# Output of tiles 0 to 11 made transposed, with x transposed as its residual

## The chip, the core and the metric

The kernel runs on one core of a Trainium2 chip. The time is that of the device in microseconds. Before the change it is 268.86 us, the median of 3 runs (268.37 to 268.89). Besides, one execution was recorded by the profiler; every duration below that is not a median comes from that one.

## What is computed

One layer with two branches over the same normalised input, summed with the input itself. S = 2048 tokens, D = 640 features, H = 32 heads of Dh = 20, F = 1536.

```python
xn = _layernorm(x)
# branch A: linear attention
q, k, v = split_heads(xn @ wqkv)
pq = einsum("bhsd,hdf->bhsf", q, w_phi)          # pk from k in the same way
phi_q = concat([softmax(pq), softmax(-pq)])      # phi_k from pk in the same way
kv  = einsum("bhsf,bhsd->bhfd", phi_k, v);  z = sum_s(phi_k)
o   = (phi_q @ kv) / (phi_q . z + 1e-6)
# branch B: gated MLP
h   = silu(xn @ w1) * (xn @ w3)
out = x + o @ wo + h @ w2
```

Inputs and output are bf16.

## The kernel before

The order of the instructions is written out by hand: each engine (TensorE, VectorE, ScalarE, GpSimd, SyncE) works through its own list in the order of the program, and waits where an operand or a buffer is not there yet. All transfers, transposing ones too, are issued by SyncE, one after the other; a transfer whose condition isn't met holds up those behind it.

Tokens are worked in 16 tiles of 128. The normalised input stands transposed in `xnT` (features by tokens). The units of work:

- `phi_unit` (L396) makes the features phi of one tile: 10 matmuls (L342, tile `pk` or `pq`) into two PSUM banks, six exponentials on ScalarE (L371), a sum (L405) and a reciprocal (L407) on VectorE, and a product on GpSimd (L408), which finishes phi.
- `kv_unit` (L481) adds one tile's phi and v into `acc`, 11 matmuls (L485).
- `glu_unit` (L439) makes one block of 128 rows of h for 512 tokens: five matmuls for the gate and five for up (L444, 512 columns each), into two PSUM banks; then a tanh on ScalarE (L455) and two products on VectorE, `gs` (L472, which reads the gate's bank) and the one into `hT` (L475, which reads the other). There are 48 such units; `fill(n)` issues the next n of them.
- `phi_transposed` (L510) transposes phi of a tile by DMA; `r_unit` (L515) multiplies it with kv (11 matmuls, L520) and `quotient` divides (L536 to L541) into `o_`; `o_transposed` (L564) transposes o of that tile by DMA into `oT`, which holds four tiles.
- `out_unit` (L575) makes the output of one tile: for each of 17 steps (12 of h with `w2`, 5 of o with `wo`), the tile's h or o is the stationary operand and 320 columns of the weight the moving one, twice, so 34 matmuls (L583) into two banks. VectorE adds the residual `xr` (L592), which `residual` has loaded, and the tile is stored.

PSUM has six banks that take turns (`bank`), and one pair beside them (`pair`).

The first loop (L822) goes over the 16 tiles for k; its passes are called i here. A pass is one `phi_unit`, one `kv_unit` (from i=2, for the tile of two passes before) and two GLU units (one in i=0). Passes 4 to 8 also fuse a block of weights and sum up one column block of the v weights on ScalarE (`column_sum`, L317). In pass 9 these sums are written to DRAM (`row`) and read back, broadcast to all partitions (`wide`, here called `less_sum`); the second transfer waits for the first. From pass 10 on, VectorE uses them in `raw_centred` (L325), one tile a pass for four passes, behind the products of that pass's GLU units.

The second loop (L846) goes over the tiles for q; its passes are called t. Pass t does `phi_unit(t)`, `r_unit(t-2)` and, from t=4, `out_unit(t-4)`; passes 0 to 3 do two GLU units each in place of the output. `w2` is loaded in pass 1. A flag (is the softmax safe without its maximum?) is made by VectorE in t=6 (L625, `flag_unit`) and read by the engines in t=8 (L878); if it is 0, a second, safer program is run, which does not happen with these inputs. The last tile's output is made in two parts, 384 and 256 columns, each stored at once.

Of the kernel before, what the change touches and what calls it, by code (L numbers as in the profile page):

```python
# [8 lines left out]
P = 128  # L9
# [3 lines left out]
def kernel(  # L13
# [17 lines left out]
    nc = tc.nc  # L31
    bf = mybir.dt.bfloat16
    f32 = mybir.dt.float32
    AF = mybir.ActivationFunctionType
    ALU = mybir.AluOpType
    AX = mybir.AxisListType

    _, S, D = A_x.shape
    H, Dh = 32, 20
    F = B_w1.shape[1]  # L40
    NST, NSC, KD, KF = S // P, S // 512, D // P, F // P
# [17 lines left out]
    x2 = A_x[0]  # L59
    out2 = out[0]  # L60
# [6 lines left out]
    def bank(name, dt=f32):  # L67
        n = 512 if dt == f32 else 1024
        return psum.tile([P, n], dt, name=name, tag="bank")
# [5 lines left out]
    xnT = one.tile([P, KD, S], bf, name="xnT")  # L75
    wkphi = one.tile([P, KD, D], bf, name="wkphi")
    wqphi = one.tile([P, KD, D], bf, name="wqphi")
    w1 = one.tile([P, KD, F], bf, name="w1")
    w3 = one.tile([P, KD, F], bf, name="w3")
# [26 lines left out]
    oT = reg_v[:, KF * D : KF * D + KD * 512].rearrange("p (c s) -> p c s", c=KD)  # L106

    def slot(i):  # L110
        return phi[:, i].rearrange("p c g f -> p (c g f)")
# [6 lines left out]
    v_raw = one.tile([P, RAW, D], f32, name="v_raw")  # L118
    less_sum = wide[:, 0:D]
    flat = v_raw[:].rearrange("p t d -> p (t d)")[0:1, 0 : P * 8]  # L120
    sums = one.tile([P, KD], f32, name="sums")
    drift = one.tile([P, RAW], f32, name="drift")
    dram = ctx.enter_context(tc.tile_pool(name="dram", bufs=1, space=bass.MemoryType.DRAM))
# [4 lines left out]
    def ld(dst, src):  # L128
        nc.sync.dma_start(out=dst, in_=src)
# [9 lines left out]
    with tc.manual_schedule():  # L139
# [193 lines left out]
        def tile_of(t):  # L333
            return slice(t * P, (t + 1) * P)
# [104 lines left out]
        def glu_unit(sc, fi, banks=None):  # L439

            gp, up = banks or (bank("gp")[:], bank("up")[:])
            for ps, w in ((gp, w1), (up, w3)):
                for c in range(KD):
                    nc.tensor.matmul(  # L444
                        ps,
                        w[:, c, fi * P : (fi + 1) * P],
                        xnT[:, c, sc * 512 : (sc + 1) * 512],
                        start=(c == 0),
                        stop=(c == KD - 1),
                    )  # L450
            return glu_done(sc, fi, gp, up)

        def glu_done(sc, fi, gp, up):
            th = work.tile([P, 512], f32, name="th")
            nc.scalar.activation(out=th[:], in_=gp, func=AF.Tanh, scale=0.5)  # L455
            return lambda: glu_product(sc, fi, gp, up, th)
# [104 lines left out]
                in1=den[:, :, None].to_broadcast([P, H, Dh]),  # L561
            )

        def o_transposed(t):  # L564
            tau = t % 4
            nc.sync.dma_start_transpose(
                out=oT[:, :, tau * P : (tau + 1) * P], in_=o_[:, t % 2]
            )

        def residual(rows):  # L570
            xr = work.tile([P, D], bf, name="xr")
            ld(xr[:], x2[rows, :])
            return xr

        def out_unit(h, ocols, xr, last=None):  # L575

            acc = [bank("acc"), bank("acc")]
            rows = [(h[:, k], w2[:, k]) for k in range(KF)]
            rows += [(oT[:, k, ocols], wo[:, k]) for k in range(KD)]
            res = work.tile([P, D], bf, name="res")  # L580

            def product(j, ps, a, b):
                nc.tensor.matmul(  # L583
                    ps[:, 0 : b - a],
                    rows[j][0],
                    rows[j][1][:, a:b],
                    start=(j == 0),
                    stop=(j == len(rows) - 1),
                )

            def result(ps, a, b):
                nc.vector.tensor_tensor(  # L592
                    out=res[:, a:b], in0=ps[:, 0 : b - a], in1=xr[:, a:b], op=ALU.add
                )

            if last is None:
                parts = [(acc[i], i * HD, (i + 1) * HD) for i in range(2)]
                for j in range(len(rows)):
                    for part in parts:
                        product(j, *part)  # L600
                for part in parts:
                    result(*part)
                return res
            for part in ((acc[0], 0, 384), (acc[1], 384, D)):
                for j in range(len(rows)):
                    product(j, *part)
                result(*part)
                a, b = part[1:]
                ld(out2[last, a:b], res[:, a:b])

        norms = one.tile([P, 8], f32, name="norms")
        flag = one.tile([P, 1], mybir.dt.int32, name="flag")

# [24 lines left out]
        def fill(n):  # L640
            for _ in range(n):
                glu_unit(*glu.pop(0))()

        def stats(t0, n):
            ln_stats(*range(t0, t0 + n))
# [176 lines left out]
        for i, t in enumerate(turns):  # L822
            phi_unit(t, wkphi, "pk")
            if i > 1:
                kv_unit(turns[i - 2], vaug[:, turns[i - 2]], acc, i == 2, False)
            if i:
                fill(1)
            if 4 <= i < 9:
                fuse(wqphi, wqT, i - 4, [bank("pf"), bank("pf")])
            fill(1)  # L830
            if i == 0:
                nc.sync.dma_start_transpose(out=wvT, in_=A_wqkv[:, 2 * D : 3 * D])
            if 4 <= i < 9:
                column_sum(i - 4)
            if i == 9:
                ld(row[:].rearrange("c p -> p c"), sums[:])
                ld(less_sum, row[:].rearrange("c p -> (c p)").partition_broadcast(P))
            if 10 <= i < 10 + RAW:
                raw_centred(i - 10)
            if i >= 12:  # L840
                norm_unit(wkphi, 0, i - 12)
        ld(wo, A_wo.rearrange("(c p) d -> p c d", p=P))

        for t in range(NST + 4):  # L846
            if t < NST:
                phi_unit(t, wqphi, "pq")
            if t < 2:
                kv_unit(turns[t - 2], vaug[:, turns[t - 2]], acc, False, t == 1)  # L850
                if t == 1:
                    kv_done([acc[:, 0], acc[:, 1]])
                    ld(w2, B_w2.rearrange("(c p) d -> p c d", p=P))
            if t < 4:
                fill(2)
            else:
                last = tile_of(NST - 1) if t == NST + 3 else None
                res = out_unit(hT[:, t - 4], tile_of(t % 4), xr, last)
            if 2 <= t < NST + 2:
                r_unit(t - 2)  # L860

            if 3 <= t < NST + 3:
                xr = residual(tile_of(t - 3))
            if 4 <= t < NST + 3:
                ld(out2[(t - 4) * P : (t - 3) * P, :], res[:])
            if t < NST:
                phi_transposed(t)
            if 2 <= t < NST + 2:
                o_transposed(t - 2)
            if t < 4:  # L870
                norm_unit(wqphi, 1, t)
            if t == 4:
                ld(listed[:], norms[:])
                ld(flat, listed[:].rearrange("p g -> (p g)").partition_broadcast(1))
            if t == 6:
                flag_unit()
            if t == 8:
                ok = nc.values_load(flag[0:1, 0:1], min_val=0, max_val=1)  # L878


# [53 lines left out]
```

## Time and profile before

| | us |
|---|---|
| median of 3 runs | 268.86 |
| the profiled execution | 268.62 |
| its span, first to last instruction | 266.8 |
| TensorE busy (modelled) | 262.0, 98% |
| VectorE busy | 195.0, 73% |
| ScalarE busy | 114.8, 43% |
| GpSimd busy | 91.1, 34% |
| queue of all transfers, share of 16 DMA engines | 46.9% |
| granted TensorE clock | 0.998 |

A matmul's reported length holds its way through the array, so matmuls overlap in the table (379 ns for one of 512 columns); what one of them costs in a dense stream is read from the starts of the matmuls that follow each other.

The span in 40 slices of 6.67 us shows where the stages lie. Each digit is the busy share of a slice in tenths:

```profile
PE   8999999999999999999999999999999999999995
PEld 7766565655555555555555555677777777777773
DVE  4779984398766777779998699976877777776341
ACT  5784444744466666344556665422222222221000
POOL 5052520055333333333444333333344444333000
PEclk9999999999999999999999999999999999999999
DMA  6998856976000000060000098455655555556931
```

Slices 0 to 7 load and normalise; the first loop runs from about 50 us (slice 7) to 144.6 us (slice 21), with nearly no transfers; the second from there to the end, with transfers at about half of what the DMA engines can hold.

### The profile page before, as it was taken

What the parts mean: (1) busy time and instruction counts of PE and PEld (TensorE: products, weight loads), DVE (VectorE), ACT (ScalarE), POOL (GpSimd) and SP (SyncE); (2) the same over time, 40 slices, a digit from 0 to 9 for tenths busy, and PEclk for the clock granted to TensorE, in tenths of its full rate; (3) what the DMA queues carried; (4) which work ended last, traced back from release to release, by engine and by line L of the source; (5) the groups of instructions that cost most, each with busy time, mean ns of one, the idle gap of its engine ahead of it and who ended that gap; (6) DMA issues with size and microseconds to landing.
All of it is one profiled execution on the core that took longest, in us unless ns stands there. A gap on an engine that the chain in (4) does not pass through costs nothing.

```text
span 266.8 us, 5294 instructions
## 1 busy us (share of the span) xinstructions
PE 262.0 (98%) x1979; PEld 167.7 (63%) x1997; DVE 195.0 (73%) x363; ACT 114.8 (43%) x348; POOL 91.1 (34%) x88
## 2 busy tenths in 40 slices
PE   8999999999999999999999999999999999999995
PEld 7766565655555555555555555677777777777773
DVE  4779984398766777779998699976877777776341
ACT  5784444744466666344556665422222222221000
POOL 5052520055333333333444333333344444333000
PEclk9999999999999999999999999999999999999999
DMA  6998856976000000060000098455655555556931
GB/s 192 248 245 185 125 118 160 333 136 119 0 0 2 0 1 3 1 176 0 0 2 0 0 270 179 114 142 144 130 128 133 149 130 128 137 147 130 155 98 55
DMA packets 69373, 29.46 MB, mean 110 GB/s; under 512 B 56287, under 2 KB 67935, under 8 KB 69344
## 3 DMA queue, kind: packets, MB, share of 16 engines
q1 hardware_dynamic: 69344, 29.08, 46.9%
q8 instruction: 17, 0.28, 0.4%
q14 instruction: 12, 0.10, 0.2%
HBM read 13.14 MB, written 2.63 MB: 59 GB/s over the span
## 4 chain that ended last, share of the span: by engine, by line
PE 98%; issue 0%; DVE 0%
PE acc L583 28%; PE up L444 19%; PE gp L444 18%; PE pq L342 8%; PE pk L342 8%; PE pv L342 6%; PE pr L520 2%; PE pkv L485 2%; PE pv L299 2%; PE pf L428 1%; PE idle L202 1%; PE pst L288 1%; PE g L461 1%; PE v L299 1%; PE gp L461 0%; PE up L461 0%
## 5 line engine op out<-in xcount | busy, mean ns | idle before, releaser
L408 POOL TENSOR_TENSOR phi<-phi,rk 128x1320 bf16<-128x1320 bf16 x32 | 77.2, 2412 | 129.0 <-DVE rk L407 102.3
L444 PEld LDWEIGHTS <-w 128*128 128x128 bf16 x460 | 43.4, 98 | 47.9 <-DMA w<-in_B_w_dram 0.2
L405 DVE TENSOR_REDUCE sk<-phi 128x66 f32<-128x1320 bf16 x32 | 48.8, 1526 | 26.7 <-ACT phi L371 25.7
L444 PE MATMUL up<-xnT,w 128*128 128x512 bf16 x227 | 57.0, 379 | 0.3
L444 PE MATMUL gp<-xnT,w 128*128 128x512 bf16 x215 | 55.8, 378 | 0.7
L583 PE MATMUL acc<-reg_v,reg_h 128*128 128x320 bf16 (+2 forms) x384 | 54.9, 299 | 0.0
L342 PEld LDWEIGHTS <-xnT 128*128 128x128 bf16 x440 | 41.7, 98 | 19.3 <-DMA xnT<-reg_h 0.5
L371 ACT ACTIVATE phi<-pq 128x360 bf16<-128x360 f32 (+2 forms) x96 | 24.8, 366 | 57.7 <-issue 34.6
L583 PEld LDWEIGHTS <-reg_h 128*128 128x128 bf16 x384 | 37.4, 98 | 14.4
L455 ACT ACTIVATE th<-gp 128x512 f32<-128x512 f32 x47 | 28.4, 603 | 27.9 <-PE gp L444 25.7
L475 DVE SCALAR_TENSOR_TENSOR reg_h<-gs,up 128x512 bf16<-128x512 bf16 x47 | 32.3, 688 | 4.8
L472 DVE SCALAR_TENSOR_TENSOR gs<-th,gp 128x512 bf16<-128x512 f32 x47 | 30.9, 658 | 4.3 <-ACT th L455 4.3
L371 ACT ACTIVATE phi<-pk 128x360 bf16<-128x360 f32 (+2 forms) x96 | 24.9, 370 | 20.0 <-PE pk L342 20.0
L592 DVE TENSOR_TENSOR res<-acc,xr 128x320 bf16<-128x320 f32 (+2 forms) x32 | 14.2, 484 | 19.0 <-PE acc L583 19.0
L583 PE MATMUL acc<-reg_w,reg_v 128*128 128x320 bf16 (+2 forms) x160 | 24.5, 299 | 0.0
L342 PE MATMUL pk<-wkphi,xnT 128*128 128x360 bf16 (+1 forms) x160 | 24.3, 299 | 0.0
L342 PE MATMUL pq<-wqphi,xnT 128*128 128x360 bf16 (+1 forms) x160 | 24.3, 299 | 0.0
L407 DVE RECIPROCAL rk<-sk 128x66 f32<-128x66 f32 x32 | 18.1, 567 | 3.2
L583 PEld LDWEIGHTS <-reg_v 128*128 128x128 bf16 x160 | 15.7, 98 | 6.1
L342 PE MATMUL pv<-reg_w,xnT 128*128 128x360 bf16 x120 | 17.4, 299 | 0.0
L228 DVE BATCH_NORM_STATS2 st<-reg_h 128x6 f32<-128x320 bf16 x32 | 13.4, 477 | 4.1 <-DMA reg_h<-in_A_x_dram 4.1
L541 DVE TENSOR_TENSOR o__77<-pr,den 128x360 bf16<-128x360 f32 (+1 forms) x32 | 14.2, 486 | 0.6
(82 smaller groups left out, 162.4 us busy)
## 6 DMA issues: line engine op xcount, KB each, us to landing
w<-in_B_w_dram SPq DMA_DIRECT2D x2, 1280.0 KB, 6.3
xr<-in_A_x_dram SPq DMA_DIRECT2D x16, 160.0 KB, 2.4
out_dram<-res SPq DMA_DIRECT2D x15, 160.0 KB, 1.8
reg_h<-in_A_x_dram SPq DMA_DIRECT2D x6, 320.0 KB, 4.7
reg_v<-in_B_w_dram SPq DMA_DIRECT2D x1, 1920.0 KB, 9.2
w<-in_B_w_dram SPq DMA_DIRECT2D x4, 320.0 KB, 4.4
reg_w<-in_A_wqkv_dram SPq DMA_DIRECT2D x5, 160.0 KB, 3.1
reg_w<-in_A_wo_dram SPq DMA_DIRECT2D x1, 800.0 KB, 7.2
```

The lines of the kernel that those rows point to most:

```text
L342: nc.tensor.matmul(ps[i][:, 0 : b - a], xnT[:, c, cols], w[:, c, a:b], start=(c == 0), stop=(c == KD - 1), skip_group_check=True,)
L371: nc.scalar.activation(out=dst[:, c0 : c0 + n, g, 0:k], in_=p.rearrange("p (c f) -> p c f", c=n), func=AF.Exp, scale=1.0 - 2.0 * g,)
L405: nc.vector.reduce_sum(out=sk[:], in_=rows, axis=AX.X)
L407: nc.vector.reciprocal(out=rk[:], in_=sk[:])
L408: nc.gpsimd.tensor_mul(out=rows, in0=rows, in1=rk[:, :, :, None].to_broadcast([P, 2 * NCH, 3, Dh]))
L444: nc.tensor.matmul(ps, w[:, c, fi * P : (fi + 1) * P], xnT[:, c, sc * 512 : (sc + 1) * 512], start=(c == 0), stop=(c == KD - 1),)
L455: nc.scalar.activation(out=th[:], in_=gp, func=AF.Tanh, scale=0.5)
L472: nc.vector.scalar_tensor_tensor(out=gs[:], in0=th[:], scalar=1.0, in1=gp, op0=ALU.add, op1=ALU.mult)
L475: nc.vector.scalar_tensor_tensor(out=hT[:, 4 * sc : 4 * sc + 4, fi, :], in0=gs[:].rearrange("p (t s) -> p t s", t=4), scalar=0.5, in1=up.r ...
L541: nc.vector.tensor_mul(out=o_[:, t % 2, Dh * h0 : Dh * h1].rearrange("p (h d) -> p h d", d=Dh), in0=p3[:, :, 0:20], in1=den[:, h0:h1, None ...
L583: nc.tensor.matmul(ps[:, 0 : b - a], rows[j][0], rows[j][1][:, a:b], start=(j == 0), stop=(j == len(rows) - 1),)
L592: nc.vector.tensor_tensor(out=res[:, a:b], in0=ps[:, 0 : b - a], in1=xr[:, a:b], op=ALU.add)
```

## The change

Tiles 0 to 11 get their output in another shape. They form three groups of four tiles (512 tokens). A group's output is made in five pieces (`out_piece`), each of 128 features by the group's 512 tokens in one PSUM bank: 17 matmuls of 512 columns, with the weight (`w2` or `wo`) as the stationary operand and h or o of the four tiles as the moving one. VectorE adds x, which has been loaded and transposed by DMA (`x_back`, one transfer for a tile), and writes bf16. When a group's five pieces are there, one DMA transposes it back (`group_back`, 20 blocks of 128 by 128) and another stores its four tiles (`group_stored`, 640 KB). Tiles 12 to 15 are made by `out_unit` as before.

Since a group's pieces can only begin when its four tiles of o are there, pieces run from pass t=7 on, one in each of t=7 to 15 and two in each of t=16, 17, 18; tile 12 follows in t=18 and tiles 13 to 15 in t=19. The passes t=4, 5 and 6, which made outputs before, get two GLU units each, so that t=0 to 6 hold two; the six units come from passes i=2, 3, 6, 9, 14 and 15 of the first loop, which keep one each. In t=0 to 5 one of the two units is made by `fill_halves(2, 2)`, where two of the five steps of gate and of up are each split in two matmuls of 256 columns. The buffers lie in `w1` and `w3`, free after the last GLU unit, and in `v_raw`. In SyncE's list, o's transpose now stands ahead of phi's. The flag is made in t=10 and read in t=12.

```diff
+    flat1 = w1[:].rearrange("p c f -> p (c f)")
+    flat3 = w3[:].rearrange("p c f -> p (c f)")
+    G = 4 * D
+    oTs = [oT] + [
+        flat3[:, i * G : (i + 1) * G].rearrange("p (c s) -> p c s", c=KD) for i in range(2)
+    ] + [oT]
+    yTs = [
+        a.rearrange("p (t c s) -> p t c s", t=4, c=KD)
+        for a in (flat1[:, 0:G], flat3[:, 2 * G : 3 * G])
+    ]
+    y = flat1[:, G : 2 * G].rearrange("p (t c s) -> p t c s", t=4, c=KD)
...
+    xTs = [
+        a.rearrange("p (c s) -> p c s", c=KD)
+        for a in (spare, flat1[:, 2 * G : 3 * G], spare)
+    ]
...
-        def o_transposed(t):
+        def o_transposed(t, group=0):
             tau = t % 4
             nc.sync.dma_start_transpose(
-                out=oT[:, :, tau * P : (tau + 1) * P], in_=o_[:, t % 2]
+                out=oTs[group][:, :, tau * P : (tau + 1) * P], in_=o_[:, t % 2]
             )
...
+        def x_back(t):
+            g, j = divmod(t, 4)
+            nc.sync.dma_start_transpose(
+                out=xTs[g][:, :, j * P : (j + 1) * P], in_=x2[tile_of(t), :]
+            )
+
+        def out_piece(g, c):
+
+            acc = bank("acc")
+            acc4 = acc[:].rearrange("p (t s) -> p t s", t=4)
+            cols = slice(c * P, (c + 1) * P)
+            for k in range(KF):
+                nc.tensor.matmul(
+                    acc4, w2[:, k, cols], hT[:, 4 * g : 4 * g + 4, k, :],
+                    start=(k == 0), stop=False,
+                )
+            for k in range(KD):
+                nc.tensor.matmul(
+                    acc[:], wo[:, k, cols], oTs[g][:, k, :], start=False, stop=(k == KD - 1),
+                )
+            nc.vector.tensor_tensor(
+                out=yTs[g % 2][:, :, c], in0=acc4,
+                in1=xTs[g][:, c].rearrange("p (t s) -> p t s", t=4), op=ALU.add,
+            )
+
+        def group_back(g):
+            nc.sync.dma_start_transpose(
+                out=y.rearrange("p t c s -> p (t c) s"),
+                in_=yTs[g % 2].rearrange("p t c s -> p (t c s)"),
+            )
+
+        def group_stored(g):
+            rows = out2[4 * g * P : 4 * (g + 1) * P, :]
+            ld(rows.rearrange("(t p) d -> p t d", p=P), y.rearrange("p t c s -> p t (c s)"))
...
+        def fill_halves(gate, up):
+
+            sc, fi = glu.pop(0)
+            gp, upp = bank("gp")[:], bank("up")[:]
+            for ps, w, whole in ((gp, w1, KD - gate), (upp, w3, KD - up)):
+                for c in range(KD):
+                    n = 1 if c < whole else 2
+                    for i in range(n):
+                        a, b = i * 512 // n, (i + 1) * 512 // n
+                        nc.tensor.matmul(
+                            ps[:, a:b],
+                            w[:, c, fi * P : (fi + 1) * P],
+                            xnT[:, c, sc * 512 + a : sc * 512 + b],
...
+                        )
+            glu_done(sc, fi, gp, upp)()
...
-            if i:
+            if i and i not in (2, 3, 6, 9, 14, 15):
                 fill(1)
...
+        pieces = {7 + i: [divmod(i, KD)] for i in range(9)}
+        pieces.update({16: [(1, 4), (2, 0)], 17: [(2, 1), (2, 2)], 18: [(2, 3), (2, 4)]})
+        xrs = {}
         for t in range(NST + 4):
...
-            if t < 4:
-                fill(2)
-            else:
-                last = tile_of(NST - 1) if t == NST + 3 else None
-                res = out_unit(hT[:, t - 4], tile_of(t % 4), xr, last)
+            if t < 7:
+                (fill_halves(2, 2) if t < 6 else fill(1))
+                fill(1)
+            for g, c in pieces.get(t, []):
+                out_piece(g, c)
+            if t in (16, 17):
+                xrs[t - 4] = residual(tile_of(t - 4))
+            outs = {18: (12,), 19: (13, 14, 15)}.get(t, ())
+            for j in outs:
+                last = tile_of(j) if j == NST - 1 else None
+                res = out_unit(hT[:, j], tile_of(j % 4), xrs[j], last)
+                if j == 12:
+                    group_back(2)
+                if j == 13:
+                    group_stored(2)
+                if j < 14:
+                    xrs[j + 2] = residual(tile_of(j + 2))
+                if last is None:
+                    ld(out2[tile_of(j), :], res[:])
             if 2 <= t < NST + 2:
                 r_unit(t - 2)
-
-            if 3 <= t < NST + 3:
-                xr = residual(tile_of(t - 3))
-            if 4 <= t < NST + 3:
-                ld(out2[(t - 4) * P : (t - 3) * P, :], res[:])
+                o_transposed(t - 2, (t - 2) // 4)
             if t < NST:
                 phi_transposed(t)
-            if 2 <= t < NST + 2:
-                o_transposed(t - 2)
+            if t in (11, 16):
+                group_back(t // 5 - 2)
+            if t in (12, 17):
+                group_stored(t // 5 - 2)
+            if 2 <= t < 6:
+                x_back(t - 2)
+            if 7 <= t < 15:
+                x_back(t - 3)
...
-            if t == 6:
+            if t == 10:
                 flag_unit()
-            if t == 8:
+            if t == 12:
                 ok = nc.values_load(flag[0:1, 0:1], min_val=0, max_val=1)
```

More of the change, by code (lines that the diff above doesn't have):

```diff
@@ L120 @@
     flat = v_raw[:].rearrange("p t d -> p (t d)")[0:1, 0 : P * 8]
+    spare = v_raw[:].rearrange("p t d -> p (t d)")[:, P * 8 : P * 8 + G // 2].bitcast(bf)
+    xTs = [
+        a.rearrange("p (c s) -> p c s", c=KD)
+        for a in (spare, flat1[:, 2 * G : 3 * G], spare)
+    ]
     sums = one.tile([P, KD], f32, name="sums")
@@ L642, in fill @@
                 glu_unit(*glu.pop(0))()
+        def fill_halves(gate, up):
[10 more added lines that the diff above has]
+                            xnT[:, c, sc * 512 + a : sc * 512 + b],
+                            start=(c == 0),
+                            stop=(c == KD - 1),
+                            skip_group_check=True,
+                        )
+            glu_done(sc, fi, gp, upp)()
         def stats(t0, n):
```

## The prediction

> **What bounds the kernel now.** I read the chain of waits first, then the same chain in order of time, then the timelines of VectorE, SyncE and TensorE around the one place where VectorE waits for a transfer, and last the granted clock by window.
>
> ```profile
> PE 98%; issue 0%; DVE 0%
> PE acc L583 28%; PE up L444 19%; PE gp L444 18%; PE pq L342 8%; PE pk L342 8%; PE pv L342 6%; PE pr L520 2%; PE pkv L485 2%; PE pv L299 2%; PE pf L428 1%; PE idle L202 1%; PE pst L288 1%; PE g L461 1%; PE v L299 1%; PE gp L461 0%; PE up L461 0%
> ```
>
> The same chain in order of time (start, length, how many matmuls):
>
> ```profile
> 14.87 1.09 PE g L461 x10
> ...
> 176.49 4.62 PE acc L583 x34
> 181.11 0.33 PE pr L520 x11
> 181.44 1.36 PE pq L342 x10
> ```
>
> TensorE is the whole chain: a microsecond leaves the time only if matmuls leave TensorE, and whatever makes TensorE wait is added in full. A pass of the second loop from t=4 is 1.36 + 4.62 + 0.33 = 6.31 us without a gap; a pass of the first loop with two GLU units is 6.01 us (below: 108.58 to 114.59).
>
> The place that matters is in the first loop. Here are SyncE, VectorE and TensorE, each with start and length:
>
> ```profile
> 103.03 0.37 SPq L129 DMA_DIRECT2D row<-sums  x1
> 112.02 0.34 SPq L129 DMA_DIRECT2D wide<-row  x1
> ...
> 115.90 0.69 DVE L475 SCALAR_TENSOR_TENSOR reg_h<-gs,up 128x512 bf16<-128x512 bf16 x1
> 117.95 1.02 DVE L325 SCALAR_TENSOR_TENSOR reg_v<-wide,drift,v_raw 128x600 bf16<-128x600 f32 x2 [1.36 <-DMA wide<-row]
> 118.88 1.52 DVE L405 TENSOR_REDUCE sk<-phi 128x66 f32<-128x1320 bf16 x1
> 120.51 0.57 DVE L407 RECIPROCAL rk<-sk 128x66 f32<-128x66 f32 x1
> 120.99 0.63 DVE L472 SCALAR_TENSOR_TENSOR gs<-th,gp 128x512 bf16<-128x512 f32 x1
> ...
> 106.42 1.24 PE L444 MATMUL gp<-xnT,w 128*128 128x512 bf16 x5
> 108.58 1.52 PE L342 MATMUL pk<-wkphi,xnT 128*128 128x360 bf16 x10
> 114.59 1.52 PE L342 MATMUL pk<-wkphi,xnT 128*128 128x360 bf16 x10
> 120.59 1.52 PE L342 MATMUL pk<-wkphi,xnT 128*128 128x360 bf16 x10
> 122.28 1.24 PE L444 MATMUL gp<-xnT,w 128*128 128x512 bf16 x4
> ```
>
> In pass i=8 ScalarE finishes the last column sum at 103.0. From there two transfers follow each other: sums to DRAM (the second is issued only at 112.02; the waits of the DMA queue put 8.5 us on it) and the broadcast back, landing about 117.9. VectorE stands idle 1.36 us for it in pass 10 and then works without a gap: 0.93 for L325, reduce, reciprocal, and the gate product of pass 11's first unit, which ends at 120.99 + 0.63 = 121.62. That product frees a PSUM bank. A pass with two units takes six banks (two for pk, two for each unit) out of six, so this bank is the one that the first gate of pass 12 writes, at 122.28. Today the margin is 122.28 - 121.62 = 0.66 us, and TensorE never sees the late transfer.
>
> **The matmuls that are exchanged.** Removed: for 12 tiles 34 matmuls of 320 columns each, 408 x 4.62/34 = 408 x 0.1359 = 55.44 us. Added: 15 pieces of 17 matmuls of 512 columns. The nearest row is a GLU unit: from 140.30 (first gate) to 144.61 (next pq) 20 such matmuls take 4.31 us, 0.2155 each; 255 x 0.2155 = 54.95 us. The columns are the same in number (130,560), so only the fixed part of 153 matmuls goes: -0.49 us. What no row shows is a moving operand in four runs of 128 columns (the 180 matmuls on hT). Bounds: no cost, or each run as a matmul of its own, as the five 128-column transposes from 7.52 to 7.79 (0.054 each; 4 x 0.055 = 0.22, +0.0045 x 180 = +0.8 us). I take none: the operand still comes at one column a step. The six units with halves hold 4 more matmuls each: 256 columns cost 1.09/10 = 0.109, two of them 0.0025 more than one of 512, x 24 = +0.06 us. Sum on TensorE: -0.43 us.
>
> **The GLU units that are moved.** Six units leave the first loop (passes 2, 3, 6, 9, 14, 15) and come back in t=4, 5, 6: nothing on TensorE by itself. But each also carries 2 products of VectorE (1.35 us) and 2.16 us of TensorE (106.42 to 108.58), and the latter was cover for the transfer above. Pass 9 lies between the column sums of pass 8 and the broadcast's use in pass 10. Counted from pass 8, transfers and VectorE's work after them stay where they are (103.0, 117.95, 121.62), while TensorE reaches the first gate of pass 12 2.16 us earlier, at 122.28 - 2.16 = 120.12. It waits there until 121.62: **+1.50 us**. VectorE's idle time grows from 1.36 to 3.52. Next behind it: the bank of the up half is free at 121.73 + 0.69 = 122.42 and wanted at 121.62 + 1.08 = 122.70; the second unit's gate at 123.01 and 123.78. So it is one wait. Bounds: the transfers a microsecond quicker or slower than in this one execution, 0.5 to 2.5 us; I take 1.5, since the DMA engines are as empty then as now.
>
> The Trainium skill ("DMA: Bandwidth & Descriptors", Rules for kernel authors) says that a transfer whose last dimension is strided becomes one descriptor per element; row<-sums writes 640 elements of 4 bytes apart, which agrees with 8.5 us for 2.5 KB and makes a shorter one unlikely.
>
> VectorE is then saturated through pass 14 (reduces at 118.88, 124.65, 130.38, 136.15 in the trace). The phi product of pass 14 on GpSimd ends at 138.51 + 2.41 = 140.92; its kv matmuls, now two short passes of 3.85 us later, come at 131.95 + 7.70 + 1.36 = 141.01. Margin 0.1; up to 0.3 us could show. Passes 2, 3 and 6 have no such transfer: kv of pass 4 comes 7.70 + 1.36 = 9.06 us after pass 2 starts and GpSimd is done 7.8 us after (pass 3 now: start 65.09, reduce at 68.11, GpSimd's product 2.36 later for 2.41).
>
> **The second loop, t=2 to 6.** VectorE needs 6.31 us there (reduce at 159.71, next at 166.02) against TensorE's 6.02, now for five passes instead of two. The margin of the first gate bank is 163.99 - 162.45 = 1.54 after t=2 and loses 0.30 a pass: 1.24, 0.94, 0.64, 0.34 when the first piece wants it in t=7. Hidden, barely; without that margin each further pass costs 0.3 us.
>
> **Pieces, t=7 to 15.** A pass is 1.36 + 3.66 + 0.33 = 5.35 us. VectorE: reduce and reciprocal 2.1, one addition of 512 (from 484 ns at 320 and 558 at 384 columns: 0.70), quotient 1.5: 4.3, hidden. SyncE now issues three transposes a pass: o 1.23, phi 1.38, and x, for which I take o's 1.23 to 1.32 (five chunks each): 3.9 of 5.35. Counted from the pass's start, r ends at 5.35 and its quotient at 7.1; o, now ahead of phi in SyncE's queue, holds it to 8.4; phi's product is ready at 7.8, so its transpose leaves at 8.4, lands 3.2 later at 11.6, and r wants it at 2 x 5.35 + 5.02 = 15.7. Margin 4.1. In t=11 three things eat into it for r of t=12 and 13: the group transpose of 20 chunks ahead of the next o and phi (1.6 us to issue by the line through 5 chunks, 1.23, and 11, 1.38; 3.5 by the weight transpose L832, 4.38 for 25 chunks; I take 1.6, whose rows also go from SBUF to SBUF), the flag's 2.0 us on VectorE, moved to t=10, which leave o and phi 1.2 late, and SyncE's reading of the flag in t=12, 1.1 (204.44 to 205.62 now). SyncE's spare 1.4 us a pass takes back part: some 2.5 us remain, 0.8 with the 3.5. TensorE does not wait. Bytes: a pass now moves 832 KB in 0.54 x 6.32 = 3.4 us of the engines; then 928 KB, 3.8 of 5.35. Removed with them: 12 loads of xr and 12 stores, off the path already. The last tile and its two stores stay as they are.
>
> **Sum.** -0.43 + 1.50 = +1.07 us. The profiled execution took 268.62 (span 266.8 and 1.82 around it): 268.62 + 1.07 = 269.7. The median shown, 268.86, is 0.24 above the profiled one.
>
> **Rivals.**
> The cover suffices: the two transfers land 1.5 us earlier or pass 12 gets another bank. For it: 14.9 us rests on one execution. Against: the queue of banks, and VectorE's 1.36 us of idle time that is already there. Then only -0.43 is left: 268.2. It decides once the broadcast lands before 116.4 on the old clock.
> SyncE's order turns into a wait: r of t=12 or 13 stands behind the group transpose. For it: the longest landing of a phi transpose in the trace is 5.8 us, 2.6 over the median, against a margin of 0.8 if the group transpose takes 3.5 to issue. It then costs 0.9 to 1.8 us beside the 1.07: 270.6 to 271.5. It decides from a margin of zero. Against: the DMA engines stay under 75%.
> The clock falls in the wait. In the windows below (stretch, length, busy times of five engines, PEclk, DMA share, GB/s) TensorE's last matmul ends at 254.51 + 9.26 = 263.8 and the granted clock is down to 0.50 by about 265.9, 2.1 us later. Were 1.5 us of waiting enough, and the clock back as late as it fell, 2.1 us at half speed would cost 1.05 more: 270.7. Against: 1.5 is less than 2.1, and the new wait is followed at once by dense matmuls.
>
> ```profile
> 264.00:265.00 1.00, 0.00 (x0) 0.00 (x0) 0.21 (x1) 0.00 (x0) 0.00 (x0) 1.00 0.03 4
> 265.00:266.00 1.00, 0.00 (x0) 0.00 (x0) 0.00 (x0) 0.00 (x0) 0.00 (x0) 0.94 0.35 90
> 266.00:266.80 0.80, 0.00 (x0) 0.00 (x0) 0.00 (x0) 0.00 (x0) 0.00 (x0) 0.50 0.00 0
> ```
>
> The Trainium skill ("TensorE: Matmul & The Clock Gate", What's actually happening) halves the clock after an idle window of about 3.4 us and raises it after a busy one; by that a fall would cost 1.7 us, an estimate. Here it fell sooner than 3.4, and by either 1.5 us is too short.
>
> **Chances.** Forecast 0.58; cover suffices 0.24; SyncE 0.12; clock 0.06. A difference under 0.2% (0.54 us) can't be told from none. Slower takes the forecast less its short waits, those under 1 us (0.51), SyncE and clock: 0.69. The covered case at 268.2 lies 0.25% under the median and 0.16% under the profiled time, so it is shared: 0.13 faster, 0.11 same; with the short waits same is 0.18. The range runs from the covered case, 268.1, to a SyncE wait of 1.5 us, 271.2; the forecast's own is 268.7 to 270.7.
>
> **What would show it.** The forecast: a TensorE wait on the gate product (now L489) in pass 12 of about 1.5 us, VectorE idle near 3.5 us at the broadcast, and 0.2155 us a matmul in the pieces. Wrong: no such wait; a wait of r on a phi transpose near t=12; pieces of more than 3.7 us; a clock under 1.00 between 115 and 130 us.

## The result, and the profile after

The changed kernel takes 271.03 us (median, 270.4 to 271.8) against 268.57 us before (268.09 to 268.89): a ratio of 1.0093, interval 1.0073 to 1.0113. It is slower by 2.5 us, inside the predicted range of 268.1 to 271.2 and well above the predicted 269.7. Its profiled execution took 270.82 us, with a span of 269.1 us; before, the span was 266.8.

The chain that ended last in the changed kernel, shares of the span by engine and then by line:

```profile
PE 87%; issue 4%; DMA 4%; DVE 3%; ACT 1%; SPq 0%; DVEq 0%
PE gp L461 14%; PE up L461 14%; PE acc L642 13%; PE pq L359 8%; PE acc L600 7%; PE pv L359 6%; PE pk L359 6%; PE acc L647 5%; PE gp L705 2%; PE up L705 2%; DMA wide<-row 2%; PE pr L537 2%; PE pv L316 2%; PE pkv L502 1%; DMA reg_w<-phi 1%
```

TensorE is no longer the whole chain. Two transfers have entered it, `wide<-row` (the broadcast of the column sums) and `reg_w<-phi` (a transpose of phi), and each stands for a wait of TensorE. In TensorE's timeline (start, length, line, operation, how many, and in brackets the idle time before and what ended it) they are the only two idle times between the start of the first loop and the end:

```profile
111.54 1.52 PE L359 MATMUL pk<-wkphi,xnT 128*128 128x360 bf16 x10
112.90 0.49 PE L502 MATMUL pkv<-reg_v,phi 128*128 128x61 bf16 x11
114.26 1.24 PE L461 MATMUL gp<-xnT,w 128*128 128x512 bf16 x5 [0.87 <-DVE gs L489]
...
217.00 0.50 PE L537 MATMUL pr<-kvr,reg_w 128*128 128x63 bf16 x11
217.34 1.52 PE L359 MATMUL pq<-wqphi,xnT 128*128 128x360 bf16 x10
...
224.12 0.51 PE L537 MATMUL pr<-kvr,reg_w 128*128 128x63 bf16 x11 [1.59 <-DMA reg_w<-phi]
```

The first is the predicted one: the first gate of pass i=12 waits for VectorE's gate product. The kv matmuls ahead of it end at 112.90 + 0.33 = 113.23 (eleven of them take 0.33 in the chain), so the wait is 1.0 us. The second is the one that the prediction's sum did not hold: `r_unit` of tile 13, in t=15, waits for phi's transpose. Undisturbed passes there are 5.37 us from one `pr` to the next (211.63 to 217.00); this one is 7.12, so the wait costs 1.75 us.

The chain in order of time through the first wait (start, length, what):

```profile
95.41 0.72 ACT junk L334 x2
...
96.15 0.38 SPq L146
...
96.58 8.04 issue
104.62 5.89 DMA wide<-row
110.51 0.03 issue
110.54 1.02 DVE reg_v L342 x2
111.56 1.45 DVE sk L422
...
113.66 0.55 DVE gs L489
```

It starts with the last column sum on ScalarE. The sums are written out (issued at 96.15; the broadcast can go only at 104.62), the broadcast lands, VectorE works off the first tile, does the reduce and reciprocal of its pass and then the gate product, whose bank TensorE wants. In VectorE's timeline the same place has this line; the idle time before it was 1.36 in the kernel before:

```profile
110.54 1.02 DVE L342 SCALAR_TENSOR_TENSOR reg_v<-wide,drift,v_raw 128x600 bf16<-128x600 f32 x2 [3.00 <-DMA wide<-row]
```

And this is SyncE's timeline ahead of the second wait (start, time to issue, line, what):

```profile
204.31 1.20 SPq L583 DMA_TRANSPOSE w<-o__77  x1
205.67 1.34 SPq L528 DMA_TRANSPOSE reg_w<-phi  x1
207.06 3.95 SPq L656 DMA_TRANSPOSE w<-w  x1
211.05 1.28 SPq L632 DMA_TRANSPOSE v_raw<-in_A_x_dram  x1
212.44 1.21 SPq L583 DMA_TRANSPOSE w<-o__77  x1
213.82 1.34 SPq L528 DMA_TRANSPOSE reg_w<-phi  x1
215.21 0.58 SPq L146 DMA_DIRECT2D out_dram<-w  x1
215.84 1.93 SPq L632 DMA_TRANSPOSE v_raw<-in_A_x_dram  x1
218.99 1.21 SPq L583 DMA_TRANSPOSE w<-o__77  x1
220.31 1.49 SPq L528 DMA_TRANSPOSE reg_w<-phi  x1
```

L656 is the transpose of group 0, and it takes 3.95 us to issue. From 204.31 on SyncE issues without a pause; the one hole, 217.77 to 218.99, is its reading of the flag, 1.2 us. Phi of tile 13 was ready at 214.42, when GpSimd ended its product; its transpose leaves at 220.31 and lands 3.8 us later, when TensorE has been waiting since 222.4.

**The account.** From the start of the first loop to the last matmul the kernel before takes 263.79 - 49.90 = 213.89 us, the changed one 265.84 - 49.49 = 216.35 (from the first `pk` to the last residual addition, which starts as the last matmul ends): +2.46. The waits make +1.02 (pass 12) and +1.75. The rest, -0.31, is what the exchange of matmuls is worth. Outside this stretch the start is 0.41 us shorter (the first loop starts at 49.3 to 51.4 in the profiles of this study, without an order by kernel), and the end, from the last matmul to the end of the span, 0.25 longer: 269.1 - 266.8 = 2.46 - 0.41 + 0.25.

The pieces themselves run as forecast: in TensorE's timeline the first starts at 175.76 and is followed by `pr` at 179.44, 17 matmuls in 3.68 us or 0.216 each, and the operand in four runs of 128 columns costs nothing that shows.

### The profile page after: what moved, and what is told of

Read it like the earlier page. It is cut to its first block, busy times and chain, and to the rows that moved or that the text cites. A ratio compares the mean times of both kernels' runs of the same rounds, so it can differ in the third digit from the quotient of the medians.

```text
span 269.1 us, 5001 instructions
## 1 busy us (share of the span) xinstructions
PE 261.1 (97%) x1842; PEld 154.6 (57%) x1868; DVE 193.4 (72%) x354; ACT 114.4 (43%) x348; POOL 91.1 (34%) x88
## 4 chain that ended last, share of the span: by engine, by line
PE 87%; issue 4%; DMA 4%; DVE 3%; ACT 1%; SPq 0%; DVEq 0%
PE gp L461 14%; PE up L461 14%; PE acc L642 13%; PE pq L359 8%; PE acc L600 7%; PE pv L359 6%; PE pk L359 6%; PE acc L647 5%; PE gp L705 2%; PE up L705 2%; DMA wide<-row 2%; PE pr L537 2%; PE pv L316 2%; PE pkv L502 1%; DMA reg_w<-phi 1%
## 5 line engine op out<-in xcount | busy, mean ns | idle before, releaser
L461 PEld LDWEIGHTS <-w 128*128 128x128 bf16 x400 | 37.8, 98 | 41.5 <-issue 1.0
L461 PE MATMUL gp<-xnT,w 128*128 128x512 bf16 x186 | 48.4, 378 | 1.5 <-DVE gs L489 0.9
L461 PE MATMUL up<-xnT,w 128*128 128x512 bf16 x197 | 49.5, 379 | 0.3
L642 PE MATMUL acc<-reg_h,reg_v 128*128 128x512 bf16 x180 | 41.3, 379 | 0.0
L642 PEld LDWEIGHTS <-reg_v 128*128 128x128 bf16 x180 | 17.4, 98 | 19.1
L650 DVE TENSOR_TENSOR w<-acc,v_raw 128x512 bf16<-128x512 f32 x10 | 6.7, 672 | 12.6 <-PE acc L647 9.6
L374 ACT CAST reg_v<-pv 128x360 bf16<-128x360 f32 (+2 forms) x36 | 9.8, 349 | 11.1 <-PE pv L359 11.1
L609 DVE TENSOR_TENSOR res<-acc,xr 128x320 bf16<-128x320 f32 (+2 forms) x8 | 3.6, 487 | 14.6 <-PE acc L600 14.6
```

The source lines that it names most:

```text
L461: nc.tensor.matmul(ps, w[:, c, fi * P : (fi + 1) * P], xnT[:, c, sc * 512 : (sc + 1) * 512], start=(c == 0), stop=(c == KD - 1),)
L642: nc.tensor.matmul(acc4, w2[:, k, cols], hT[:, 4 * g : 4 * g + 4, k, :], start=(k == 0), stop=False,)
```

## The experiments

Theories before the experiments: the first wait exists because pass 9 lost 2.16 us of TensorE's work, which covered the two transfers; the second because the issue of the group's transpose and the flag (made by VectorE in t=10, read by SyncE in t=12) make SyncE late. Rivals are named with each. Runs made together share the runs of the kernel before, and ratios are compared only within such a group: e1 to e4, e5 to e8, e9 to e12.

### Moving one thing at a time: e1 to e4

e1 lets pass 12 have the short turn in place of pass 9:

```diff
-            if i and i not in (2, 3, 6, 9, 14, 15):
+            if i and i not in (2, 3, 6, 12, 14, 15):
```

> The unit that pass 9 of the first loop lost is given back to it and taken from pass 12. Theory: the 1.0 us that TensorE waits on the gate product in pass 12 (113.2 to 114.3) is there only because pass 9 no longer covers the two transfers of the column sums. It goes; VectorE's idle time at the broadcast falls from 3.0 back to about 1.0 to 1.4 us; the wait of r on phi's transpose near t=15 stays; 1.0 us less than the changed kernel: about 270.0. Rival: short passes as such saturate VectorE, and the wait moves to another pass of the first loop: within 0.3 us of 271.0.

Measured: 272.89 us, ratio 1.0125 (1.0092 to 1.0158). It was not faster, and the rival came true. TensorE's idle times in the first loop and right behind it:

```profile
116.55 1.24 PE L461 MATMUL gp<-xnT,w 128*128 128x512 bf16 x5 [0.19 <-DVE gs L489]
...
127.81 1.24 PE L461 MATMUL gp<-xnT,w 128*128 128x512 bf16 x5 [1.26 <-DVE gs L489]
...
135.62 0.50 PE L502 MATMUL pkv<-reg_v,phi 128*128 128x61 bf16 x11 [0.28 <-POOL phi L425]
```

The wait at pass 12 fell to 0.19 us, which speaks for the cover. How much cover it is shows beside e2 (next), where pass 9 is short and the two transfers take as long (15.8 us from issue to use there, 15.9 here). VectorE's first use of the sums in e1 and in e2:

```profile
112.83 1.02 DVE L342 SCALAR_TENSOR_TENSOR reg_v<-wide,drift,v_raw 128x600 bf16<-128x600 f32 x2 [2.32 <-DMA wide<-row]
112.62 1.02 DVE L342 SCALAR_TENSOR_TENSOR reg_v<-wide,drift,v_raw 128x600 bf16<-128x600 f32 x2 [4.44 <-DMA wide<-row]
```

The idle times lie 2.12 us apart, and a GLU unit is 2.16 us of TensorE. But two passes later there is one of 1.26, and a kv wait behind it. Pass 12 is one of the four in which VectorE also works off the sums: 0.93 for that, 2.1 for reduce and reciprocal and 1.35 for one unit are 4.4 us, where a short pass gives it 3.85. So the short pass had no room on VectorE either; the choice of pass was bad, and the lag was moved, not paid off. The wait of r stayed, as expected (listed as 0.17 and 1.43 us for tiles 12 and 13).

e2 leaves the first loop alone and moves the flag behind the critical place:

```diff
-            if t == 10:
+            if t == 16:
                 flag_unit()
-            if t == 12:
+            if t == 18:
                 ok = nc.values_load(flag[0:1, 0:1], min_val=0, max_val=1)
```

> The flag is made in t=16 and read in t=18, in place of 10 and 12; all else as in the changed kernel. Theory: r of t=15 waits 1.6 us for phi's transpose because SyncE is late: it stands in line behind the flag's 2.0 us on VectorE in t=10, the group transpose that takes 3.95 us to issue in t=11 and its own reading of the flag in t=12 (1.2 us). Without the flag's two parts (some 2.3 us together) phi's transpose of t=13 leaves at about 218 in place of 220.3 and lands before r wants it at 222.5: about 1.6 us less, 269.4; the wait in pass 12 of the first loop stays. Rival: the group transpose itself holds the DMA engines (0.9 of them are busy from 205 to 220), so phi lands late all the same: under 0.6 us less.

e3 moves the transpose of group 0 in its place. In e3 and e4 group 1 is transposed into the shared buffer before group 0 is stored, so group 0's rows of the output get group 1's; the work is the same.

```diff
-            if t in (11, 16):
-                group_back(t // 5 - 2)
-            if t in (12, 17):
-                group_stored(t // 5 - 2)
+            if t in (15, 16):
+                group_back(0 if t == 15 else 1)
+            if t in (16, 17):
+                group_stored(0 if t == 16 else 1)
```

> Group 0 is transposed back in t=15 and stored in t=16, in place of 11 and 12; the flag stays at 10 and 12. Theory: taking 3.95 us of issue out of the stretch of SyncE between t=11 and t=13 is enough: no wait of r, about 1.6 us less, 269.4. Rival: the flag alone makes SyncE late, and then r still waits about as long: under 0.6 us less.

Measured: e2 270.92 us, ratio 1.0075 (1.0041 to 1.0109); e3 271.24 us, 1.0094 (1.0059 to 1.0129). In both the wait of r is gone from TensorE's timeline, and both times hardly show it, since the first wait had grown: 2.31 us in e2 and 2.25 in e3. TensorE's only idle time behind the start in e2:

```profile
116.34 1.24 PE L461 MATMUL gp<-xnT,w 128*128 128x512 bf16 x5 [2.31 <-DVE gs L489]
```

and e2's chain in order of time, to be held against 8.04 and 5.89 above:

```profile
97.22 9.12 issue
106.34 6.26 DMA wide<-row
```

From issuing the sums to VectorE's use of them it is 15.8 us here (96.79 to 112.62), 14.4 in the changed kernel's profile (96.15 to 110.54), with the same instructions up to that point. The difference of 1.4 us in the two small transfers goes into the first wait one for one, so these two runs can't be read by their medians; what they show is that either part of SyncE's load, taken out alone, ends the second wait. They also answer the rival that busy DMA engines hold phi up. In e2 the group's transpose stands where it was and the engines are 0.89 to 1.00 busy from 207 to 222 us, and r doesn't wait all the same.

The longer transfers go with the chip. The record has e1 to e4 and e9 to e12 on one chip and e5 to e8 on another; from the issue of the sums to that of the broadcast it is 9.15 to 9.55 us in the eight profiles of the first and 8.44 to 8.57 in the four of the second (8.47 in the changed kernel's own, whose chip is not on record). Why they differ is not known.

e4 does all three moves (pass 12 short, flag late, group 0 in t=15 and 16).

> The unit from pass 12, the flag in 16 and 18, and group 0 transposed in t=15, together. Theory: both waits go and what is left is the exchange of matmuls, -0.3 us: TensorE without a gap from the first loop to the end, about 268.2 to 268.4, 0.1% under the kernel before. Rival: a third cost is hidden behind the two waits (the end of the span, the x transposes, or the pieces): still 0.5 us or more above the kernel before.

Measured: 271.51 us, ratio 1.0084 (1.0062 to 1.0107). There is no wait of r, but the waits of e1's first loop are back: 0.28 at pass 12, 1.25 two passes later, 0.28 for kv. That sent me to another way of giving the transfers time.

### Both waits apart and together: e5 to e8

e5 is the changed kernel once more, beside the other three.

> The changed kernel once more, beside the next three. In experiment e2 the two transfers of the column sums took 15.8 us from the last sum to the landing and TensorE's wait in pass 12 was 2.3 us, against 14.4 and 1.0 in the changed kernel's own profile. Theory: both waits are here again, the one in pass 12 as long as the transfers of this execution make it (1.0 to 2.3 us), the one of r near 1.6: 271.0 to 272.3.

Measured: 271.28 us, ratio 1.0091 (1.0062 to 1.0120); the waits are where they were (listed as 1.04 and 1.49 us).

e6 leaves pass 9 short and uses the sums a pass later:

```diff
-            if 10 <= i < 10 + RAW:
-                raw_centred(i - 10)
+            if 11 <= i < 11 + RAW:
+                raw_centred(i - 11)
```

> The changed kernel with VectorE's use of the broadcast (raw_centred) in passes 11 to 14 of the first loop in place of 10 to 13; no unit is moved. Theory: the wait in pass 12 is the late broadcast alone. With 6.0 us more cover VectorE doesn't stand idle for it, TensorE has no wait in the first loop, and the time falls by just that wait, 1.0 to 2.3 us under e5; the wait of r stays. Rival, after e1, where the wait came back in pass 14: the short passes themselves saturate VectorE, and a wait of 1 us or more stays in the first loop.

Measured: 270.62 us, ratio 1.0068 (1.0041 to 1.0094). In VectorE's timeline the first use of the sums has no idle time ahead of it:

```profile
114.28 1.01 DVE L342 SCALAR_TENSOR_TENSOR reg_v<-wide,drift,v_raw 128x600 bf16<-128x600 f32 x2
```

The broadcast, issued at 105.52, landed 5.9 us later at 111.4, well ahead of 114.28. TensorE's first wait is gone; the second is as in the changed kernel, in TensorE's timeline:

```profile
224.00 0.51 PE L537 MATMUL pr<-kvr,reg_w 128*128 128x63 bf16 x11 [1.54 <-DMA reg_w<-phi]
```

The first loop takes 132.06 - 50.31 = 81.75 us, 1.03 less than in the changed kernel (132.27 - 49.49 = 82.78).

e7 is e6 with e2's edit of the flag as well.

> As e6, and the flag made in t=16 and read in t=18 (as e2). Theory: no wait of TensorE is left between the first loop and the end; only the exchange of matmuls remains, -0.3 us: 0.1% under the kernel before, where that has no wait of its own. Rival: a third cost outside the two waits: 0.5 us or more above the kernel before.

Measured: 268.17 us, ratio 0.9992 (0.9979 to 1.0005). No wait is left in either loop; TensorE's `pr` of t=14 and t=15 follow each other by the undisturbed 5.37:

```profile
215.81 0.50 PE L537 MATMUL pr<-kvr,reg_w 128*128 128x63 bf16 x11
...
221.18 0.50 PE L537 MATMUL pr<-kvr,reg_w 128*128 128x63 bf16 x11
```

From the first loop's start to the last matmul it takes 262.89 - 49.33 = 213.56 us: 0.33 under the kernel before. So the two waits were the whole loss in that stretch, and nothing else is hidden in the transposed output.

e8 goes the other way: the kernel before, with nothing changed but one GLU unit taken from pass 9 to pass 0.

```diff
-            if i:
+            if i != 9:
                 fill(1)
```

> The kernel before, with one GLU unit moved from pass 9 to pass 0 of the first loop (0 then has two, 9 one) and nothing else: no transposed output, the same matmuls. Theory: this alone brings the wait in pass 12, 1.0 to 2.3 us in its trace and in its time, 269.7 to 271.2. Rival: the wait needs the other short passes or the new second loop: within 0.3 us of the kernel before.

Measured: 269.61 us, ratio 1.0038 (1.0020 to 1.0056), some 1.0 us. TensorE's timeline has the wait:

```profile
123.39 1.24 PE L444 MATMUL gp<-xnT,w 128*128 128x512 bf16 x5 [0.98 <-DVE gs L472]
```

and VectorE's the longer idle time:

```profile
119.67 1.01 DVE L325 SCALAR_TENSOR_TENSOR reg_v<-wide,drift,v_raw 128x600 bf16<-128x600 f32 x2 [3.11 <-DMA wide<-row]
```

The short pass 9 alone, without a single transposed output, makes the first wait.

### What the second wait is made of: e9 to e12

e9 is e6 with only the reading of the flag moved; VectorE still makes it in t=10.

```diff
-            if t == 12:
+            if t == 18:
                 ok = nc.values_load(flag[0:1, 0:1], min_val=0, max_val=1)
```

> The column sums used a pass later (as in e6), and of the flag only the reading moved, from t=12 to t=18; it is still made by VectorE in t=10. The wait of r in t=15 is some 1.5 us in e6. Theory: SyncE's list is full without a gap from the o transpose of t=11 (204.1 in e6) to the phi transpose of t=13 (220.3), and the reading takes 1.2 us of it, so 0.3 us of the wait stays, and the time is 1.2 us under e6's against the same before: +0.9 us (ratio 1.003). Rival: the late start of that stretch, which VectorE's 2.0 us for making the flag sets, is the whole cause and SyncE's reading hides behind a transfer: the wait stays at 1.5 and the ratio at 1.007.

Measured: 270.04 us, ratio 1.0047 (1.0033 to 1.0061), between the two. TensorE's timeline:

```profile
217.25 0.51 PE L537 MATMUL pr<-kvr,reg_w 128*128 128x63 bf16 x11 [0.30 <-DMA reg_w<-phi]
...
223.37 0.51 PE L537 MATMUL pr<-kvr,reg_w 128*128 128x63 bf16 x11 [0.59 <-DMA reg_w<-phi]
```

0.89 us of listed waiting stay of 1.54, where the theory left 0.3. SyncE's list accounts for most of the difference: phi of tile 13 leaves at 219.59 here and at 220.34 in e6, 0.75 sooner and not 1.2, because the phi transpose of tile 11 and the group's transpose behind it took longer to issue (2.46 + 3.38 us here, 2.34 + 3.13 in e6). They also make the wait one pass earlier, for phi of tile 12, which stands in the list ahead of the reading. So the reading is a part of the cause, but not the whole; whether it is worth its full 1.2 us of time this run does not show.

e10 is e6 with the flag where the change has it and group 0 transposed in t=14 and stored in t=15.

```diff
-            if t in (11, 16):
-                group_back(t // 5 - 2)
-            if t in (12, 17):
-                group_stored(t // 5 - 2)
+            if t in (14, 16):
+                group_back(0 if t == 14 else 1)
+            if t in (15, 17):
+                group_stored(0 if t == 15 else 1)
```

> The column sums used a pass later (as in e6), the flag where the change has it, and group 0 transposed back in t=14 and stored in t=15 rather than in t=11 and 12. Theory: the 3.1 to 4.3 us that SyncE needs to issue the group's transpose then lie behind the o and phi of t=13, and r of t=15 doesn't wait: ratio 0.999, as in e7. Rival one: the wait only moves to r of t=16 or 17, by 0.5 to 1.5 us: 1.001 to 1.005. Rival two: the flag alone is the cause and the group's transpose none: 1.5 us of waiting stay, 1.007.

Measured: 268.71 us, ratio 0.9993 (0.9982 to 1.0003), with no wait of r in any pass. SyncE's timeline:

```profile
213.79 1.21 SPq L583 DMA_TRANSPOSE w<-o__77  x1
...
221.70 4.21 SPq L656 DMA_TRANSPOSE w<-w  x1
```

The group's transpose is no shorter, 4.21 us, but by now the flag's share has been paid back and nothing is late behind it. The first line is o of t=13: 213.79, in place of 218.99 in the changed kernel.

e11 is e7 with whole units in place of the six with halves; e12 is e7 again.

```diff
-                (fill_halves(2, 2) if t < 6 else fill(1))
+                fill(1)
```

> e7 (sums used a pass later, flag made in t=16 and read in t=18) with whole units in place of the six with halves. By the sum of the prediction 24 matmuls fewer give 0.06 us: ratio 0.0002 under e7's, not to be told from it. Rival: the halves are there because a whole unit makes VectorE's lag show in t=2 to 6: then TensorE waits there and the time is above e7's by 0.3 us or more.

> e7 once more, to see if the mended kernel beats the one before: with both waits gone the exchange of matmuls alone is left, -0.3 us by the trace of the changed kernel and -0.4 by the prediction's sum: ratio 0.9985 to 0.9995. If pieces and transfers cost something that no wait shows, it is 1.000 or more.

Measured: e11 268.55 us, ratio 0.9992 (0.9982 to 1.0003); e12 268.73 us, 0.9995 (0.9984 to 1.0006). Neither has a wait in the loops. From the first loop's start to the last matmul e11 takes 263.65 - 50.15 = 213.50 us, 0.06 less than e7, e10 and e12 (213.56 each): the six units with halves cost what 24 matmuls more were said to, and VectorE's lag doesn't show without them.

So the four mended versions (e7, e10, e11, e12) lie 0.05% to 0.08% under the kernel before, and every interval holds 1: they win back the loss, and none is shown to beat the kernel before. The traces say why the 0.33 us don't arrive. From the last matmul to the end of the span it is 3.0 us in the kernel before and in e8, and 3.2 to 3.3 in every profile of the changed order (e7: 266.2 - 262.89 = 3.3), with the same last store ahead of it. What makes this difference was not tried.

## Why the prediction was right and wrong

**The exchange of matmuls: right.** -0.43 us was predicted with the halves in it, -0.33 measured (e7). A matmul of a piece costs 0.216 us, not 0.2155, and the operand in four runs is free, as taken.

**The wait in pass 12: right in place, mechanism and cover; only its size was off.** 1.5 us was predicted, 1.0 measured in the profiled execution, with VectorE idle for 3.00 us and not 3.52. The difference is the transfers: 14.4 us from issue to use where the profile of before had 14.9. In e2, with 15.8, the listed wait is 2.31 in place of 0.87. Both lie within the 0.5 to 2.5 given. That the lost cover is the cause is shown twice: e8 makes the wait with it alone, and e6 ends the wait without giving the cover back, by wanting the sums later.

**The margins called thin: right where they were only tight.** Neither the kv matmuls of pass 14 nor the second loop's t=2 to 6 show a wait in the changed kernel. Pass 14's product on GpSimd ends at 131.12 + 2.41 = 133.53 and its kv matmuls start at 133.63: the margin of 0.1 is there as predicted. In e1 and e4, where that product ends some 0.5 us later against TensorE's passes, they did wait, 0.28 us.

**"Some 2.5 us remain ... TensorE does not wait": this step failed.** It is the margin of r for tiles 12 and 13, by which the sum held no wait of r at all; 1.75 us came. The prediction had phi's transpose leave 8.4 us after its pass starts, with 4.1 us to spare. Pass 13 starts at 206.61, so 215.0 was due; it left at 220.31, 5.3 late, and landed 0.6 later than the 3.2 taken. 5.3 + 0.6 - 4.1 = 1.8, the wait that was measured. The 5.3 by parts, from the SyncE lines above:

- the group's transpose, 3.95 us to issue. I took 1.6, from a line through transposes of 5 and 11 chunks; the three in the changed kernel took 2.98, 3.15 and 3.95. The higher bound of 3.5, from a transpose out of DRAM, was the better row. Part of the 3.95 may not be the group's own: in e2, e6, e7, e9 and e12 group 0's transpose took 3.13 to 3.40, but phi's right ahead of it 1.96 to 2.46 in place of 1.34; in e3, where no group stands there, that phi took 2.51 all the same. What adds 0.6 to 1.2 us to one issue in t=11 is not known.
- the store of the group behind it, 0.58, and a longer issue of the next x, 1.93 in place of 1.28. Neither was in the working.
- the flag: its making holds o of t=11 to 204.31, 1.3 after the 202.98 at which the quotient was due (195.88 + 7.1), and its reading takes 1.2. Both were counted, about rightly.
- against these 7.7 us SyncE's spare time of two passes is 2 x (5.37 - 3.9) = 2.9; the gaps of 0.04 to 0.17 between two issues take half a microsecond of it.

The margin itself was not added up rightly. By the terms named, 4.1 - 1.6 - 1.2 - 1.1 and two passes' spare of 1.4 each make 3.0 us, not 2.5, and 1.1, not 0.8, with the 3.5. What had been left out is more than the 1.1: the store 0.58, the longer issue of x 0.65, the gaps 0.5 and the later landing 0.6 are 2.3 us, and the group's transpose took 0.45 more than the 3.5. e10 shows that the group's transpose decides by its place alone, e2 and e7 that the flag's two parts together do, e9 that the reading alone is not enough. The group's transpose and the flag fit into SyncE's list each by itself, not together.

The Trainium skill ("DMA: Bandwidth & Descriptors", Rules for kernel authors) advises to coalesce many small transfers into one large one. In sum the trace agrees: one transpose of 20 chunks takes 2.98 to 3.95 us to issue, and four of 5 chunks would take 4 x 1.2 = 4.8, an estimate that no run tried. What cost the time here is that the large one held up everything behind it in the same list; e10 puts it where nothing is due.

**The argument against that rival fell too.** "The DMA engines stay under 75%" came from the bytes. These windows of the changed kernel give stretch, length, busy times of five engines, granted clock, DMA share and GB/s:

```profile
205.00:210.00 5.00, 5.00 (x38) 2.85 (x37) 3.78 (x9) 1.55 (x6) 2.41 (x1) 1.00 0.92 104
210.00:215.00 5.00, 4.95 (x37) 2.78 (x37) 3.83 (x8) 1.54 (x6) 2.41 (x1) 1.00 0.91 201
215.00:220.00 5.00, 5.00 (x39) 2.73 (x37) 4.15 (x8) 1.19 (x5) 2.41 (x1) 1.00 0.91 236
220.00:225.00 5.00, 3.35 (x25) 1.61 (x25) 3.04 (x6) 0.38 (x3) 2.26 (x1) 1.00 0.94 167
```

The engines are over 90% busy, also in the first stretch, which moves only 104 GB/s. Before, the same stretches had 0.41 to 0.60 at 112 to 146 GB/s. What is moved in the first stretch are transposes alone; plain copies in the same trace (the broadcast and the load of `wo`, 109 to 110.5 us) kept the engines 0.97 busy at 299 GB/s. A transposed byte kept them busy nearly three times as long as a copied one, so bytes were the wrong measure. That busy engines alone don't make the wait is seen in e2; whether they lengthened the group's issue or phi's landing was not tried.

**The clock: right.** The granted clock stayed at 1.00 through waits of 1.0, 1.75 and, in e2, 2.31 us. The Trainium skill ("TensorE: Matmul & The Clock Gate", What's actually happening) has the clock fall after an idle window of about 3.4 us; with waits this short the runs agree.

**The verdict.** Slower had the greatest chance, for a reason that holds. The size was wrong because the rival "SyncE's order turns into a wait" came true. It had been priced well, at 0.9 to 1.8 us beside the 1.07 (1.75 measured), but given a chance of 0.12 on a margin that was not there. -0.33 + 1.02 + 1.75 is 2.4, where -0.43 + 1.50 was predicted. That the time lies inside the range is in part luck: with a first wait of the predicted 1.5 us it would have been some 271.5, above the 271.2.

## What to carry to other kernels

Work taken from one pass is also cover taken from every transfer that spans that pass; look for the transfer whose wait already shows on another engine, even where it costs nothing yet, and want its result later rather than giving the cover back. A queue that issues in order is an engine with a budget per pass: add up every issue that lies between the moved instruction and the next one that somebody waits for, stores and register reads too, and put a long one where nothing behind it is due. Where two rows bound a cost and the higher leaves a margin under a microsecond, the margin is not there.

## What the runs showed that was not expected

- The time to issue a transpose is not a straight line in its size: 1.2 us for 5 chunks of 128 by 128, mostly 1.36 for 11, 2.96 to 4.35 for 20 over all runs. In the changed kernel the transposes of 20 chunks landed 4.9 to 6.3 us after their issue.
- Two small transfers that follow each other (2.5 KB out, then broadcast back) took 14.4 to 14.9 us from issue to use in the profiles of before, after, e5 and e8, and 15.8 to 16.0 in e1 to e4, which ran on another chip than e5 and e8.
- Reading one flag into SyncE's register held its queue for 1.2 us.
- The granted clock doesn't follow the length of an idle time alone: it stayed at 1.00 through 2.31 us of waiting (e2) and in the changed kernel's profile to the end, 3.2 us after the last matmul, while in the profile of before it had fallen 2.1 us after it.
